# Queries from halves of w_q, and finer key loads at the change of layers, in a two-layer decode kernel

## The chip, the cores and the metric

The kernel runs on one core of one Trainium2 chip. The metric is the device time of one execution in microseconds (us); of the kernel before there are three runs, and their median is taken. All stages below are told in us from the start of the span of one profiled execution.

## The reference

Two equal layers, each an attention block and a feed-forward block, run one decode step for 4 batch entries (B) with model width 512 (D). x is [4, 1, 512] in bf16.

```python
q = layernorm(x) @ wq                       # [4, 512] @ [512, 4096]: 32 query heads of 128
p = softmax(q . k_cache * 128**-0.5)        # 8 key heads, 4 query heads each, 8192 keys
x = x + (p . v_cache) @ wo
h = layernorm(x)
x = x + (silu(h @ w_gate) * (h @ w_up)) @ w_down     # 512 -> 1792 -> 512
# ... and both once more with the same weights and the same caches
```

Nearly all the bytes are the caches: keys and values are 64 MB each, and both layers read them.

## The kernel before, in words

**Tiles.** The work of attention is cut into 16 pairs in each layer; a pair is one batch entry and two key heads. The keys of a pair (here K0 to K15) are 4 MB, 32 KB on each of the 128 partitions, and so are its values (V0 to V15). A tile of this size lies in a slot of the on-chip tensor `kvf`, in 8 blocks of 4 KB a partition. There are four slots (0 to 3), and a fifth one, `QS`, in which w_q lies (4 MB, loaded once as two halves, `wq0` and `wq1`) until layer 1 has made its queries from it; after that QS is a slot as the others. The feed-forward weights are loaded into slot 1 in layer 0 and slot 3 in layer 1.

**One pair.** VectorE (DVE) transposes each block of keys in place (`turn`, L488, 8 instructions). TensorE (PE) makes scores from each block with four matmuls of 512 columns (`scores`, L512). Then DVE takes the maximum (`max_p`, L518), PE turns it (L523), DVE and PE spread it (L526, L549 or L554), ScalarE makes the exponentials (L559), DVE transposes them (L576), and PE multiplies them with the values (`values`, L643).

**Order of the work.** Each engine runs its instructions in the order in which the Python program emits them. Two lists defer work: `blocks` holds score and value blocks until their estimated times exceed a lag, and `line` holds the steps of a softmax. For the second pair of layer 1 the lag is 15 (`AHEAD`), so that all its eight `turn`s stand on DVE ahead of the first pair's `max_p`.

**Order of the loads.** All loads are issued by SyncE (SP), in one fixed list (`cmds`, from L346). `pump` (L405) issues the next command as soon as the program order reaches a point where its blocks are in the set `free`; `freed(s, a, b)` adds blocks a to b of slot s and calls `pump`. Each load waits, on SP, for the readers of the blocks that it writes. A command that isn't ready keeps back all that follow.

**Dependences.** `_Sync` records by name the last writer and the readers of each resource. An instruction waits for the writer of what it reads, and for the writer and the readers of what it writes. The record knows no subset of a name, and no later correction: the writer of `wq0` is whichever instruction last named it in its writes.

**The change of layers.** Layer 0 works through pairs 0 to 15, layer 1 through 15, 14, 13, 12, 0, ... 11. K15 (slot 0, transposed), V15 (slot 3) and V14 (slot 2) stay for layer 1. Blocks 6 and 7 of K13 stay too: `hold` (L444) transposes them into four banks of PSUM in layer 0, and in layer 1 transposes them back into QS (L452), where the rest of K13 is loaded. Because blocks 6 and 7 of QS lie in w_q, the copy back waits for both names `WQ` (L451). In `load`, the first load into QS also takes both of these names as written (L430).

The order at the change is: feed-forward block of layer 0 (`ffn`), `center` (mean and variance), `qproj` (128 small matmuls L839, of which 64 ahead of and 64 behind the variance's matmul L826), then the two copies back, `freed(QS, 0, 6)`, and the pairs. K14 is loaded into slot 1 as the feed-forward weights there are used up, in parts of blocks 0-3 (after w_gate), 3-4 (after w_up) and 4-8 (after w_down). Then come K13 into QS (blocks 0-4 and 4-6), K12 into slot 0 in two halves as the scores of K15 free it, V13 into slot 1 in two halves as the scores of K14 free it, K0 into slot 3 after V15's products, V12 into QS, K1 into slot 2, and so on in a ring of the five slots.

In `qproj`, the matmuls run head by head, with the four parts of D (`kt`) inside; each one reads `wq0` (kt 0, 1) or `wq1` (kt 2, 3).

Of the kernel before, what the change touches and what calls it, by code (L numbers as in the profile page):

```python
# [103 lines left out]
def bass_interleave_layers__gqa_block_cached__swiglu_ffn__decode_kernel(  # L104
# [40 lines left out]
    with ExitStack() as es:  # L145
# [50 lines left out]
        def room(s, a, b):  # L196
            return [f"s{s}.{q}" for q in range(a // BW, (b - 1) // BW + 1)]
# [48 lines left out]
        def bank(k):  # L246
            return ps[:, k * BANKF:(k + 1) * BANKF]
# [87 lines left out]

        ends = lambda it, s: [(it, s, 0, QH), (it, s, QH, NB - 1), (it, s, NB - 1, NB)]
        half = lambda it, s: [(it, s, q, q + NB // 2) for q in range(0, NB, NB // 2)]

        def placed(seq, ring, parts):
            out = []  # L340
            for i, it in enumerate(seq):
                s = ring[i % len(ring)]
                out += parts[i](it, s) if i in parts else [(it, s, 0, NB)]
            return out
# [10 lines left out]

        us = order[1]
        s = W_SLOT[0]
        cmds += [(K(1, us[1]), s, 0, 3), (K(1, us[1]), s, 3, 4), (K(1, us[1]), s, 4, NB)]
        cmds += [(K(1, us[2]), QS, 0, NB // 2), (K(1, us[2]), QS, NB // 2, NB - 2)]
        seq = loads(1, 3)  # L360
        ring = (0, 1, 3, QS, 2)
        cmds += placed(seq, ring, {0: half, 1: half, len(seq) - 1: ends})
        assert W_SLOT[1] == ring[len(seq) % len(ring)]
        cmds += [(("W", 1), W_SLOT[1], 0, NB), (("W+", 1), W_SLOT[1], NB, NB + 1)]

# [58 lines left out]
        def load(it, a, b, sm):  # L424
            kind, L, u = it
            s = slot_of[it]
            gp, bt = pair_gb(u)
            src = (A_k_cache if kind == "K" else A_v_cache)[bt, 2 * gp:2 * gp + 2, :, :].rearrange(
                "h (p t) d -> (h p) (t d)", t=TT)
            over = WQ if s == QS and not q_gone else []  # L430
            q_gone.update(over)
            T.dma("sp", kv[:, s, a * BW:b * BW], src[:, a * BW:b * BW], sm,
                  writes=[f"s{s}.{q}" for q in range(a, b)] + over)
# [398 lines left out]

        def qproj(L, u):
            at, name = place("ln", 0, Hq * B)
            for h in range(Hq):
                if h == Hq // 2:
                    deviation(lsc_sb, "lsc")
                for kt in range(KT):
                    T.op("pe", lambda e: e.matmul(at[:, h * B:(h + 1) * B],  # L839
                                                  lhsT=wq_sb[:, kt, h * Dh:(h + 1) * Dh],  # L840
                                                  rhs=xn[:, kt * B:(kt + 1) * B],
                                                  start=(kt == 0), stop=(kt == KT - 1)),
                         reads=[f"wq{kt // 2}", "xn"], writes=[name], sig=(kt == KT - 1))
            T.op("dve", lambda e: e.tensor_tensor(qT, at.rearrange("p (h b) -> p b h", b=B),
                                                  rstd[:].unsqueeze(2).to_broadcast([P, B, Hq]), ALU.mult),
                 reads=[name, "rstd"], writes=["qT"] + OT)

            pick = ident.rearrange("p (c j e) -> p c j e", c=2, e=2)
            ob, oname = place("q", 0, NQR)
            ob = ob.rearrange("p (c b g r) -> p c b g r", c=4, b=B, g=GP)  # L850
            qv = qT.rearrange("p b (g h r) -> p b g h r", h=2, r=REP)
            for c in range(4):
                for a in range(NA):
                    T.op("pe", lambda e: e.matmul(ob[a * QB:(a + 1) * QB, c],
                                                  lhsT=pick[:, c // 2, :, c % 2],
                                                  rhs=qv[:, :, :, a // 2, :], start=True, stop=True),
                         reads=["qT", "ident"], writes=[oname], sig=(a == NA - 1))
            place_q(L, u, "dve", ob, [oname])
            T.op("dve", lambda e: e.tensor_copy(qr, ob), reads=[oname], writes=["qr", "made"])

        def ffn(L):
            s = W_SLOT[L]
            gb, ub = OBK[0], SBK[0]
            gT = bank(gb)[:, 0:FO * B]
            uT = bank(ub)[:, 0:FO * B]
            fb = lambda ap: ap.rearrange("p (f b) -> p f b", b=B)
            rb = rstd[:].unsqueeze(1).to_broadcast([P, FO, B])
            rooms = {"wg": room(s, 0, O_WU), "wu": room(s, O_WU, O_WD), "wd": room(s, O_WD, O_WD + FO * D)}
            names = {"wg": ["wg"], "wu": ["wu0", "wu1", "wu2"]}
            for at, wname, bk in ((wg_at, "wg", gb), (wu_at, "wu", ub)):  # L870
                for fo in range(FO):
                    if bk == gb and fo == FO // 2:
                        deviation(zero_sb, "zero")
                    f = base(L, fo)
                    for kt in range(KT):
                        T.op("pe", lambda e: e.matmul(bank(bk)[:, fo * B:(fo + 1) * B],  # L876
                                                      lhsT=at(s, kt, *f),
                                                      rhs=xn[:, kt * B:(kt + 1) * B],
                                                      start=(kt == 0), stop=(kt == KT - 1)),
                             reads=rooms[wname] + names[wname] + ["xn"], writes=[f"pb{bk}"],  # L880
                             sig=(fo == FO - 1 and kt == KT - 1))
                freed(s, *((0, 3) if wname == "wg" else (3, 4)))
            T.op("dve", lambda e: e.tensor_tensor(fb(gr), fb(gT), rb, ALU.mult),
                 reads=[f"pb{gb}", "rstd"], writes=["gr", "pb"])
            T.op("act", lambda e: e.activation(eg, gr, ACTF.Exp, scale=-1.0), reads=["gr"], writes=["eg"])
            T.op("dve", lambda e: e.tensor_tensor(fb(gw), fb(gr), rb, ALU.mult), reads=["gr", "rstd"], writes=["gw"])
            T.op("dve", lambda e: e.tensor_scalar(eg, eg, 1.0, None, op0=ALU.add), reads=["eg"], writes=["eg"])
            T.op("dve", lambda e: e.reciprocal(eg, eg), reads=["eg"], writes=["eg"])
            T.op("dve", lambda e: e.tensor_tensor(eg, gw, eg, ALU.mult), reads=["gw", "eg"], writes=["eg"])
            T.op("dve", lambda e: e.tensor_tensor(hT, eg, uT, ALU.mult), reads=[f"pb{ub}", "eg"], writes=["hT"])  # L890
            if L == 1:
                x_rows(1)
                for i, (a, b, _) in enumerate(WDS[1]):
                    for fo in range(a, b):
                        for j in range(NA):
                            o = s * SL + O_WD + fo * D + j * P
                            T.op("pe", lambda e: e.matmul(quarter(j), lhsT=hT[:, fo * B:(fo + 1) * B],
                                                          rhs=kvf[:, o:o + P], start=False, stop=(fo == FO - 1)),
                                 reads=["hT", f"wd{i}"] + rooms["wd"], writes=[f"part{j}"],
                                 sig=(fo == b - 1))  # L900
                freed(s, 4, NB)
                return
            for j, (a, b, _) in enumerate(WDS[0]):
                k = OBK[0] if j else SBK[1]
                for nt in range(KT):
                    for fo in range(a, b):
                        T.op("pe", lambda e: e.matmul(bank(k)[:, nt * B:(nt + 1) * B],
                                                      lhsT=wd_at(s, fo, nt),
                                                      rhs=hT[:, fo * B:(fo + 1) * B],
                                                      start=(j < 2 and nt == 0 and fo == a),  # L910
                                                      stop=(j in (0, NW - 1) and nt == KT - 1 and fo == b - 1)),
                             reads=["hT", f"wd{j}"] + rooms["wd"], writes=[f"pb{k}"], sig=(fo == b - 1))
                if not j:
                    add_to_x(bank(k)[:, 0:XB], f"pb{k}")
            freed(s, 4, NB)
            add_to_x(bank(k)[:, 0:XB], f"pb{k}")


# [10 lines left out]
        for L in range(2):  # L929
# [6 lines left out]
            if L:  # L936
                for q in (NB - 2, NB - 1):
                    hold(q, True)
                freed(QS, 0, NB - 2)
            todo = [("K", 0)]  # L940
            for i in range(1, NP - 1):
                todo += [("K", i), ("V", i - 1)]
# [49 lines left out]
```

## Time and profile before

| | |
|---|---|
| Runs | 648.29, 649.24, 649.81 us, median 649.24 |
| The profiled execution | 648.29 us, of which its span is 646.5 us |
| PE busy | 425.6 us (66%) |
| DVE busy | 430.1 us (67%) |
| ScalarE, GpSimd busy | 41.2 us, 11.1 us |
| Read from memory | 272.90 MB, 422 GB/s over the span |
| Granted TensorE clock, mean | 0.876 |

A busy time is a sum over stages that differ, so it doesn't say by itself which engine sets the end. The page's row of 40 slices shows the share of time in which the 16 DMA engines had packets, and the GB/s that they moved; the chain of waits follows the work that ended last back through whatever released each step. "Landing" is the time from a load's issue on SP until its semaphore is complete. The loads at the change of layers stand like this in the profile, each from SP's own timeline and the landing of that one issue:

| Load | KB | issued at | landed after, us |
|---|---|---|---|
| K14, blocks 0-3 | 1536 | 345.06 | 9.4 |
| K14, 3-4 | 512 | 348.35 | 7.3 |
| K14, 4-8 | 2048 | 351.19 | 9.4 |
| K13, 0-4 and 4-6 | 2048, 1024 | 356.71 and next | 9.0, 11.1 |
| K12, 0-4 | 2048 | 363.87 | 10.6 |
| K12, 4-8 | 2048 | 367.36 | 12.1 |
| V13, 0-4 | 2048 | 372.50 | 11.8 |
| V13, 4-8 | 2048 | 375.98 | 13.2 |
| K0 | 4096 | 378.16 | 20.8 |

### The profile page before, as it was taken

To read this page: it belongs to the slowest core of one execution; us is meant where nothing else is said; L and a number is where in the kernel's file an instruction comes from. 1 tells how busy PE (TensorE), PEld (TensorE's weight loads), DVE (VectorE), ACT (ScalarE), POOL (GpSimd) and SP (SyncE) were. 2 spreads that over 40 slices of the span, in tenths; PEclk is the share of its full clock that TensorE was granted. 3 is DMA by queue.
4 is the path that set the end of the run, shared out by engine and by line. 5 is a ranking of instruction groups with operands and counts; after the bars stand their busy time and mean duration, and the time that the engine had idled before them with its cause. 6 is when DMAs were issued, how large, how long until landed. Compare 5 with 4: busy or idle time off the path is not lost.

```text
span 646.5 us, 7503 instructions
## 1 busy us (share of the span) xinstructions
PE 425.6 (66%) x3128; PEld 173.1 (27%) x3128; DVE 430.1 (67%) x706; ACT 41.2 (6%) x117; POOL 11.1 (2%) x43
## 2 busy tenths in 40 slices
PE   2574466556766755767757987777665576657878
PEld 2221122212322212222226332222222222222225
DVE  1585467566776666777852878888766677766953
ACT  1000000000000000001010010000000000000110
POOL 0000000000000000000000000000000000000000
PEclk9996896789787999878985799999878997789977
DMA  9999999999999999999999999999999999999996
GB/s 363 445 423 416 442 429 430 426 435 433 426 430 435 430 425 436 435 422 436 434 407 409 396 435 434 434 429 423 442 427 426 433 438 424 431 440 423 430 417 268
DMA packets 14129, 273.37 MB, mean 423 GB/s; under 512 B 1416, under 2 KB 1424, under 8 KB 5264
## 3 DMA queue, kind: packets, MB, share of 16 engines
q1 hardware_dynamic: 14096, 272.91, 99.0%
q8 instruction: 24, 0.39, 0.2%
q14 instruction: 9, 0.07, 0.0%
HBM read 272.90 MB, written 0.00 MB: 422 GB/s over the span
## 4 chain that ended last, share of the span: by engine, by line
DMA 61%; DVE 26%; PE 9%; issue 3%; SPq 0%; ACT 0%; DVEq 0%
DMA kvf<-in_A_k_cache_dram 49%; DVE kvf L488 20%; DMA kvf<-in_A_v_cache_dram 10%; PE ps L512 3%; DVE pT L576 3%; PE ps L643 2%; DMA kvf<-in_B_w_down_dram 2%; DVE pb L693 2%; PE ps L839 1%; DVE pb L689 0%; PE ps L876 0%; DVE scr L703 0%; DVE kvf L452 0%; PE ps L759 0%; SPq L93 0%
## 5 line engine op out<-in xcount | busy, mean ns | idle before, releaser
L512 PE MATMUL ps<-kvf,zq 128*128 128x512 bf16 x1024 | 298.0, 426 | 181.1 <-DVE kvf L488 174.3
L488 DVE STREAM_TRANSPOSE kvf<-kvf 128x1024 f32<-128x1024 f32 x246 | 289.8, 1219 | 108.6 <-DMA kvf<-in_A_k_cache_dram 107.7
L512 PEld LDWEIGHTS ps<-kvf,zq 128*128 128x128 bf16 x1024 | 90.6, 105 | 350.9 <-DVE kvf L488 257.8
L643 PE MATMUL ps<-kvf,pT 128*32 128x512 bf16 x960 | 66.7, 400 | 1.4 <-DVE pT L576 0.8
L559 ACT ACTIVATE pb<-ps,tiny 128x512 bf16<-128x512 f32 x32 | 22.0, 688 | 531.8 <-DVE tiny L557 495.2
L576 DVE STREAM_TRANSPOSE pT<-pb 64x512 bf16<-64x512 bf16 x60 | 41.2, 687 | 3.1 <-ACT pb L559 2.0
L518 DVE TENSOR_REDUCE tiny<-ps 128x1 f32<-128x512 f32 x32 | 22.0, 687 | 31.6 <-PE ps L512 31.6
L693 DVE SCALAR_TENSOR_TENSOR pb<-ps,tiny,pb 128x128 f32<-128x128 f32 x104 | 36.5, 351 | 5.1 <-PE ps L643 1.3
L643 PEld LDWEIGHTS ps<-kvf,pT 128*32 128x32 bf16 x960 | 20.8, 98 | 31.9 <-issue 15.7
L698 PEld LDWEIGHTS ps<-sel,pb 128*128 128x128 f32 x64 | 15.4, 258 | 21.3 <-DVE pb L693 14.0
L502 POOL TENSOR_TENSOR zq<-scr,tiny 128x64 bf16<-128x64 bf16 x30 | 9.0, 300 | 564.8 <-PE ps L512 564.8
L526 DVE TENSOR_REDUCE mrm<-ps 1x8 f32<-1x128 f32 x32 | 8.8, 275 | 14.2 <-PE ps L523 14.2
L698 PE MATMUL ps<-sel,pb 128*128 128x8 f32 x64 | 12.7, 272 | 8.1 <-DVE pb L693 8.1
L549 PEld LDWEIGHTS ps<-mrm,tiny 128*128 128x128 f32 x60 | 12.0, 205 | 8.6 <-DVE scr L703 3.2
L759 PE MATMUL ps<-wo_sb,scr 128*4 128x512 bf16 x48 | 11.0, 379 | 1.5 <-DVE scr L728 1.5
L689 DVE TENSOR_SCALAR pb<-ps,tiny 128x128 f32<-128x128 f32 x32 | 10.1, 315 | 2.6 <-PE ps L643 2.6
L549 PE MATMUL ps<-mrm,tiny 128*128 128x16 f32 x60 | 9.3, 231 | 3.1 <-ACT mrm L561 3.1
L839 PE MATMUL ps<-xn,kvf 128*128 128x4 bf16 x256 | 7.6, 166 | 3.8 <-DMA kvf<-in_A_wq_dram 3.0
L561 ACT ACTIVATE mrm<-head,tiny 128x8 f32<-128x8 f32 x32 | 9.6, 301 | 1.0
L523 PE MATMUL ps<-identf,tiny 128*1 128x128 f32 x32 | 8.6, 270 | 0.2 <-DVE tiny L518 0.2
L839 PEld LDWEIGHTS ps<-xn,kvf 128*128 128x128 bf16 x256 | 7.6, 106 | 4.0 <-DMA kvf<-in_A_wq_dram 3.1
L876 PE MATMUL ps<-xn,kvf 128*128 128x4 bf16 x224 | 7.3, 169 | 1.8 <-DMA kvf<-in_B_w_up_dram 1.4
(83 smaller groups left out, 113.9 us busy)
## 6 DMA issues: line engine op xcount, KB each, us to landing
kvf<-in_A_k_cache_dram SPq DMA_DIRECT2D x28, 4096.0 KB, 30.8
kvf<-in_A_v_cache_dram SPq DMA_DIRECT2D x27, 4096.0 KB, 32.9
kvf<-in_A_v_cache_dram SPq DMA_DIRECT2D x4, 2048.0 KB, 20.0
kvf<-in_A_k_cache_dram SPq DMA_DIRECT2D x4, 2048.0 KB, 10.0
kvf<-in_A_wq_dram SPq DMA_DIRECT2D x2, 2048.0 KB, 9.8
wo_sb<-in_A_wo_dram SPq DMA_DIRECT2D x4, 1024.0 KB, 40.6
kvf<-in_B_w_gate_dram SPq DMA_DIRECT2D x2, 1792.0 KB, 24.5
kvf<-in_A_v_cache_dram SPq DMA_DIRECT2D x2, 1536.0 KB, 34.8
```

The costliest lines, as they stand in the source:

```text
L488: T.op("dve", lambda e: e.transpose(w, w), reads=[f"s{s}.{q}"], writes=[f"s{s}.{q}"])
L512: T.op("pe", lambda e: e.matmul(bank(bk)[:, 0:SW], lhsT=zq[:, z0:z0 + P], rhs=w[:, :, c // 2, :, c % 2], start=(q == 0 and c == 0), stop=( ...
L518: T.op("dve", lambda e: e.tensor_reduce(mx[:], bank(bk)[:, 0:SW], AX.X, ALU.max), reads=[f"pb{bk}"], writes=["mx"])
L549: T.op("pe", lambda e: e.matmul(at, lhsT=ones, rhs=mrm[:, i * H2:(i + 2) * H2], start=True, stop=True), reads=[f"m8{i}", "rsm", "onesf"], ...
L559: T.op("act", lambda e: e.activation(pb[:], bank(bk)[:, 0:SW], ACTF.Exp, bias=nm, accum_out=rs), reads=[f"pb{bk}", "nm"], writes=PB + ["rs"])
L576: T.op("dve", lambda e: e.transpose(dst, pb[hp]), reads=["pb", "row"], writes=[name])
L643: T.op("pe", lambda e: e.matmul(bank(k)[j * QB:(j + 1) * QB, q0 * Dh:q1 * Dh], lhsT=p_t[:, t, h, :], rhs=v[:, q0:q1, t, :], start=((last o ...
L689: T.op("dve", lambda e: e.tensor_scalar(into, o, own[:, q:q + 1], None, op0=ALU.mult), reads=[f"pb{k}", "own"], writes=["row"] if last els ...
L693: T.op("dve", lambda e: e.scalar_tensor_tensor(into, o, own[:, q:q + 1], into, op0=ALU.mult, op1=ALU.add), reads=[f"pb{k}", "own", iname], ...
L698: T.op("pe", lambda e: e.matmul(at, lhsT=into, rhs=sel[:], start=True, stop=True), reads=[iname, "sel"], writes=[name])
L759: T.op("pe", lambda e: e.matmul(bank(OUTB)[0:B, 0:D], lhsT=oT[:, h, :], rhs=wo_sb[:, h, :], start=(gp == groups[L][0] and r == 0), stop=(g ...
L839: T.op("pe", lambda e: e.matmul(at[:, h * B:(h + 1) * B], lhsT=wq_sb[:, kt, h * Dh:(h + 1) * Dh], rhs=xn[:, kt * B:(kt + 1) * B], start=(k ...
```

## The change

1. `qproj` runs by halves of w_q: 64 matmuls with kt 0 and 1 over all heads, then the variance, then 64 with kt 2 and 3. One accumulation covers the whole tile: it starts at the first matmul and stops at the last. Between the halves, layer 1 calls `freed(QS, 0, 4)`; after the copies back only blocks 4 to 6 are freed.
2. The first load into each half of QS takes over the name of that half alone.
3. K14 loads as blocks 0-3, 3-4, 4-6, 6-8; w_down's names are kept by part, and blocks 4-6 of slot 1 are freed after the first part of w_down.
4. K12 loads as four parts of two blocks.

```diff
+        twos = lambda it, s: [(it, s, q, q + 2) for q in range(0, NB, 2)]
...
-        cmds += [(K(1, us[1]), s, 0, 3), (K(1, us[1]), s, 3, 4), (K(1, us[1]), s, 4, NB)]
+        cmds += [(K(1, us[1]), s, a, b) for a, b in ((0, 3), (3, 4), (4, 6), (6, NB))]
...
-        cmds += placed(seq, ring, {0: half, 1: half, len(seq) - 1: ends})
+        cmds += placed(seq, ring, {0: twos, 1: half, len(seq) - 1: ends})
...
-            over = WQ if s == QS and not q_gone else []
+            over = [w for i, w in enumerate(WQ) if s == QS and a // (NB // 2) == i and w not in q_gone]
...
-            for h in range(Hq):
-                if h == Hq // 2:
+            for c in range(2):
+                if c:
                     deviation(lsc_sb, "lsc")
-                for kt in range(KT):
...
+                for h in range(Hq):
+                    for kt in (2 * c, 2 * c + 1):
...
+                                                      start=(kt == 0 and h == 0), stop=(kt == KT - 1 and h == Hq - 1)),
+                             reads=[f"wq{c}", "xn"], writes=[name], sig=(kt % 2 == 1 and h == Hq - 1))
+                if L and not c:
+                    freed(QS, 0, NB // 2)
...
-            rooms = {"wg": room(s, 0, O_WU), "wu": room(s, O_WU, O_WD), "wd": room(s, O_WD, O_WD + FO * D)}
+            rooms = {"wg": room(s, 0, O_WU), "wu": room(s, O_WU, O_WD)}
+            for j, (a, b, _) in enumerate(WDS[L]):
+                rooms[f"wd{j}"] = room(s, O_WD + a * D, O_WD + b * D)
...
                 if not j:
+                    freed(s, 4, 6)
                     add_to_x(bank(k)[:, 0:XB], f"pb{k}")
-            freed(s, 4, NB)
+            freed(s, 6, NB)
...
                 for q in (NB - 2, NB - 1):
                     hold(q, True)
-                freed(QS, 0, NB - 2)
+                freed(QS, NB // 2, NB - 2)
```

More of the change, by code (lines that the diff above doesn't have):

```diff
@@ L834, in qproj @@
             at, name = place("ln", 0, Hq * B)
-            for h in range(Hq):
-                if h == Hq // 2:
+            for c in range(2):
+                if c:
                     deviation(lsc_sb, "lsc")
-                for kt in range(KT):
[L839 to L843, printed above, removed]
+                for h in range(Hq):
+                    for kt in (2 * c, 2 * c + 1):
+                        T.op("pe", lambda e: e.matmul(at[:, h * B:(h + 1) * B],
+                                                      lhsT=wq_sb[:, kt, h * Dh:(h + 1) * Dh],
+                                                      rhs=xn[:, kt * B:(kt + 1) * B],
+                                                      start=(kt == 0 and h == 0), stop=(kt == KT - 1 and h == Hq - 1)),
+                             reads=[f"wq{c}", "xn"], writes=[name], sig=(kt % 2 == 1 and h == Hq - 1))
+                if L and not c:
+                    freed(QS, 0, NB // 2)
             T.op("dve", lambda e: e.tensor_tensor(qT, at.rearrange("p (h b) -> p b h", b=B),
@@ L898, in ffn @@
                                                           rhs=kvf[:, o:o + P], start=False, stop=(fo == FO - 1)),
-                                 reads=["hT", f"wd{i}"] + rooms["wd"], writes=[f"part{j}"],
+                                 reads=["hT", f"wd{i}"] + rooms[f"wd{i}"], writes=[f"part{j}"],
                                  sig=(fo == b - 1))
@@ L911, in ffn @@
                                                       stop=(j in (0, NW - 1) and nt == KT - 1 and fo == b - 1)),
-                             reads=["hT", f"wd{j}"] + rooms["wd"], writes=[f"pb{k}"], sig=(fo == b - 1))
+                             reads=["hT", f"wd{j}"] + rooms[f"wd{j}"], writes=[f"pb{k}"], sig=(fo == b - 1))
                 if not j:
+                    freed(s, 4, 6)
                     add_to_x(bank(k)[:, 0:XB], f"pb{k}")
-            freed(s, 4, NB)
+            freed(s, 6, NB)
             add_to_x(bank(k)[:, 0:XB], f"pb{k}")
```

## The prediction

> **What bounds the kernel now.** I read the page's DMA rows first, then the chain, then the change of layers by its chain, SP's issues, DVE's and PE's timelines, and windows.
>
> ```profile
> DMA  9999999999999999999999999999999999999996
> ...
> q1 hardware_dynamic: 14096, 272.91, 99.0%
> ...
> DMA 61%; DVE 26%; PE 9%; issue 3%; SPq 0%; ACT 0%; DVEq 0%
> ```
>
> The loads' packets fill 99.0% of 16 engines' span. Outside the start and the end no slice shows DMA short of work, so the end is when the last bytes are through plus the tail behind them. A delay of any engine costs nothing as long as the DMA queue holds bytes, and everything once it is empty. In layer 1 compute needs less per pair than DMA: after the change of layers it is behind, and from 437.77 it waits for keys again (DVE's timeline, second line below). So I count one thing only: how long the queue stands empty at the change of layers.
>
> The chain there:
>
> ```profile
> 357.64 0.41 DVE scr L859
> 358.06 2.29 DVE kvf L452 x2
> 360.35 9.01 DVE kvf L488 x8
> 369.36 0.59 DVE tiny L518
> 369.99 0.27 PE ps L523
> 370.26 0.87 PE ps L512 x4
> 371.13 0.31 PE ps L554 x2
> 371.44 4.46 PE ps L512 x20
> ```
> ```profile
> 437.77 2.37 DVE L488 STREAM_TRANSPOSE kvf<-kvf 128x1024 f32<-128x1024 f32 x2 [2.38 <-DMA kvf<-in_A_k_cache_dram]
> ```
>
> From 357.98 (DVE's own timeline) DVE copies back K13's blocks 6 and 7 (L452), turns K14's eight blocks (L488), and only then takes K15's maximum (L518). PE has K14's third and fourth block behind the matmul that waits for this maximum (L523). V13's first half is issued when the fourth is scored, at 372.50. So a delay of the copies is a delay of V13's load, one for one.
>
> **The change part by part.**
>
> *Queries by halves.* The same 128 matmuls with 64 ahead of the variance and 64 behind it: nothing in layer 1. In layer 0 the third matmul waits until 13.47 for the second half of w_q; now 64 run in that wait, some 1.8 us of PE. But DVE's first `turn` waits for K0 until 24.25, idle 5.42 us before it: nothing. It would give 1.8 us if keys landed by 17.
>
> *K14's last part cut in two.* Blocks 4-6 can be issued after the first w_down part, at about 349.9 instead of 351.19. The loads in front land until 355.7, so nothing is gained. Three more issues in all, at 0.33 us each on SP, which mostly waits: nothing.
>
> *K13's first half issued between the halves of qproj.* At about 354.5 instead of 356.71. What this can repair is in the windows:
>
> ```profile
> 352.00:356.00 4.00, 3.65 (x114) 3.56 (x114) 0.61 (x4) 0.56 (x2) 0.00 (x0) 0.50 1.04 419
> 356.00:360.00 4.00, 3.27 (x47) 1.62 (x44) 2.79 (x5) 0.00 (x0) 0.00 (x0) 0.50 0.93 336
> ```
>
> The last two columns are DMA's share and GB/s. Share 0.93 over 4 us is 0.3 us lost. By landings, K13's first half came 5.1 us after K14 (360.6 to 365.7), where a full queue takes 4.9 us for 2 MB (379.5 to 384.3 to 389.2). K12's finer parts similarly fill a queue that runs thin around 366. From 360.6 to 379.5 the queue moved 7 MB in 18.9 us; at 4.9 us for 2 MB that is 17.2. So the gain is between 0 and 1.7 us, and without the next step it would be the whole effect of the change.
>
> *The wait that comes with it.* `load` takes over the name `wq0` as its write. Until now this load was issued after the copies back, which wait for both names and so found w_q's own loads, long landed. Now it is issued ahead of them, and the writer of `wq0` is K13's first half. The instruction order of the changed kernel shows it: the first L452 copy on DVE waits for the semaphore of that load, where it waited for w_q's. The copied blocks don't need these bytes; the wait is by name only.
>
> When does it land? K14 lands at 360.6 as before; 2 MB at 4.9 us gives **365.5**. DVE stands still from 357.98 to 365.5: **7.5 us**. Queued behind are the eight turns, K15's maximum, and so PE's third block. PE itself goes on with K15's scores (no need of DVE) until 367.3, so K12's four parts are issued in time, the last at 367.4 as before. They land at 365.5 + 2.5 (K13, 1 MB) + 9.8 (4 MB) = 377.8, or 379.5 if the loss around 370 stays. This is all that the queue holds.
>
> *When V13 comes.* 372.50 + 7.5 = 380.0 if PE runs as fast. But it idles between K14's second block (about 371) and the maximum (369.99 + 7.5 = 377.5), some 6 us. Where that happens now:
>
> ```profile
> 79.35 3.17 PE L512 MATMUL ps<-kvf,zq 128*128 128x512 bf16 x7 [7.63 <-DVE kvf L488]
> ...
> 458.49 3.47 PE L512 MATMUL ps<-kvf,zq 128*128 128x512 bf16 x8 [5.03 <-DVE kvf L488]
> ```
> ```profile
> 76.00:80.00 4.00, 0.65 (x2) 0.28 (x3) 1.95 (x2) 0.00 (x0) 0.00 (x0) 0.50 1.03 442
> ```
>
> After 7.63 us and 5.03 us of idling the granted clock is 0.50 for the first 3.3 us of work (column before DMA's). Four matmuls of a block take 1.03 us at full clock and 1.7 at half (0.43 each in the 358 to 362 stretch). Two blocks: +1.4. V13's first half is issued at **381.4**, between 380.0 and 382.
>
> What it then takes: no row shows a full-size load into an idle queue in mid-run. Bounds: 4.9 us of transfer plus 1.0 from issue to first packet (0.74 to 1.78 in the start's windows) is 5.9; the first half of w_q, issued into the empty queue at the start, landed after 7.8, with DMA slow in its first microseconds (180 and 147 GB/s). I take 7.0, between them. 381.4 + 7.0 = 388.4 against 372.50 + 11.8 = 384.3: **+4.1 us**. The bounds give 380.0 + 5.9 = +1.6 and 382 + 7.8 = +5.5.
>
> *After that.* V13's second half is issued 3.5 to 5 us later, under the first one's transfer. DVE and PE are some 9 us late by then. V12's load goes from 389.06 to 398; K0's, ahead of it, would land at 384.3 + 4.1 + 4.9 + 9.8 = 403.1, so the queue stays filled. Compute's slack of 2.38 us at 437.77 grows by 19.4 (DMA for a pair) less 14.9 (405.46 to 420.15 in the chain) with each pair, so the lag beyond DMA's, 5 us, is gone by 460, and the end moves by DMA's delay alone.
>
> *1 MB loads.* Six are new. K13's 1 MB part, in 8 KB rows, landed 2.5 us after the load in front (365.7 to 368.2), which is the rate of 2 MB parts; I take 0.1 us for all. The Trainium skill's page "DMA: Bandwidth & Descriptors" (section "Measured (HBM→SBUF, 128 partitions, SWDGE, issued from GpSimd)") speaks against the change: a 1 MB transfer takes 6.15 us, 16 MB take 79.0, so it says to batch to 1 MiB and more. By that, six loads would be an estimated 7.3 us dearer than as part of large ones; the row above doesn't bear it out for loads queued behind others.
>
> Sum: stall +4.1, small parts +0.1; the thin places' gain lies ahead of the empty queue and is lost in it. 648.29 + 4.2 = 652.5 for the profiled execution, which was the fastest of the three runs; the median is 0.95 above it. I put the forecast between, **653.0**.
>
> **Rivals.**
> - *The stall is mostly covered* (0.14). If V13 restarts quickly, PE stays at full clock, and the engines whose packets lag (K12's second half was as late as 379.5) have less to lose: +0.8 to +1.6, that is 650 to 651. For: landings there are later than byte counts ask. Against: the queue has nothing behind K12.
> - *Faster* (0.05). One mechanism: the earlier K13 and K12 parts keep the queue full, and the stall ends before the queue does: -1.7, or 647.5. It decides at V13's issue: it must come some 1.5 us before K12's last bytes, by 376, so the stall must stay below 3.5 us, and K13's half land by 361.5. K14, in front of it, lands at 360.6 and 2 MB take 4.9, so this needs the wait not to bind at all.
> - *The queue empties twice* (0.10). If PE stays at half clock for all of K14's last four blocks (16 matmuls, 6.9 us instead of 3.5), V13's second half comes too late as well, and V12's after it: +6 to +9, 654.5 to 658.
> - *Small loads run slow* (0.03). The slowest 2 us with weights in small parts moved 398 GB/s against 430: 6 MB then cost 15.8 us instead of 14.6, +1.2 on top, 654.2. Its rule is the page named above.
> - *The half isn't released early* (0.01): SP would issue K13 as before, without the wait by name: 649.
>
> **How the numbers follow.** The forecast has the rest, 0.67: 651.0 to 654.5 by its bounds. The range takes in the covered stall and part of the double gap: 650.0 to 656.5. About 0.2% (1.3 us) is what a measurement of this kernel can tell from no change. Faster 0.05; within it 0.09 (half of the covered stall, the unreleased half, a little of the forecast's low end); slower 0.86.
>
> **What would show it.** In the changed profile's DVE timeline, an idle time of 7 to 8 us ahead of the first L452, ended by a key load; PE idle some 6 us ahead of L523, and a clock of 0.5 after it; V13's issue at 380 to 382; a window of 2 to 5 us with DMA's share far below 1 between 376 and 384; none of this at 357. Later issues should be 4 to 9 us late, and the keys' wait at 437 should come near 442. I am wrong if the idle time ahead of L452 is missing, or if DMA's share stays near 1 through 376 to 384.

## The result, and the profile after

| | before | after |
|---|---|---|
| Runs, us | 647.47 to 649.81 (5) | 654.68 to 655.70 (5) |
| Median, us | 648.29 | 655.11 |
| The profiled execution (its span) | 648.29 (646.5) | 654.68 (652.9) |
| Ratio after to before | | 1.01, 95% interval 1.0085 to 1.0114 |

The changed kernel is about 1% slower, 6.8 us by the medians. Between the two profiled executions the difference is 6.4 us, in the span as in the whole.

The page of the changed kernel: DMA's busy share in 40 slices, the loads' queue (packets, MB, share of 16 engines' span), and the shares of the chain that ended last.

```profile
DMA  9999999999999999999999959999999999999997
...
q1 hardware_dynamic: 14528, 272.91, 98.1%
...
DMA 62%; DVE 26%; PE 8%; issue 3%; SPq 0%; ACT 0%; ACTq 0%; DVEq 0%
```

The bytes are the same and the share is 98.1% instead of 99.0%. Between the start and the end one digit has changed: slice 24 (375.4 to 391.7 us) fell from 9 to 5. The windows there, with PE, PEld, DVE, ACT and POOL busy, the granted clock, DMA's share and GB/s:

```profile
356.00:360.00 4.00, 3.27 (x49) 1.62 (x47) 0.85 (x3) 0.00 (x0) 0.00 (x0) 0.50 1.03 426
...
372.00:376.00 4.00, 0.00 (x0) 0.00 (x0) 4.00 (x5) 0.00 (x0) 0.00 (x0) 0.91 0.90 371
376.00:380.00 4.00, 2.33 (x7) 0.87 (x7) 1.90 (x3) 0.00 (x0) 0.00 (x0) 0.50 0.11 47
380.00:384.00 4.00, 4.00 (x16) 1.68 (x16) 1.59 (x4) 1.08 (x3) 0.00 (x0) 0.73 0.31 66
384.00:388.00 4.00, 3.81 (x41) 1.30 (x39) 1.79 (x3) 0.00 (x0) 0.30 (x1) 1.00 0.94 401
```

The thin place of before at 356 to 360 (share 0.93) is full, and from 376 to 384 next to nothing is read. What stood in the way is in the chain of the changed kernel (start, us, what):

```profile
354.69 10.94 DMA kvf<-in_A_k_cache_dram
365.63 0.02 issue
365.65 2.38 DVE kvf L453 x2
368.03 9.01 DVE kvf L489 x8
377.04 0.59 DVE tiny L519
377.63 0.04 issue
377.67 0.37 PE ps L524
378.05 1.71 PE ps L513 x4
```

It is the chain of before, moved by 7.6 us, and a load now stands at its head: K13's first half, issued at 354.69 and landed at 365.63. DVE's and PE's own timelines give the idle time ahead of the first copy back and ahead of the matmul that turns K15's maximum (in brackets: idle, and who ended it):

```profile
365.65 2.38 DVE L453 STREAM_TRANSPOSE kvf<-ps 128x1024 f32<-128x1024 f32 x2 [7.49 <-DMA kvf<-in_A_k_cache_dram]
```
```profile
377.67 0.37 PE L524 MATMUL ps<-identf,tiny 128*1 128x128 f32 x1 [6.28 <-DVE tiny L519]
377.84 1.91 PE L513 MATMUL ps<-kvf,zq 128*128 128x512 bf16 x4
```

SP issued V13's first half at 382.17 (372.50 before). It landed 7.3 us later, at 389.4 (384.3 before).

### The profile page after: what moved, and what is told of

The parts are those of the page before. It is cut to its first block, busy times and chain, and to the rows that moved or that the text cites. A ratio compares the mean times of both kernels' runs of the same rounds, so it can differ in the third digit from the quotient of the medians.

```text
span 652.9 us, 7505 instructions
## 1 busy us (share of the span) xinstructions
PE 426.8 (65%) x3126; PEld 174.4 (27%) x3128; DVE 430.2 (66%) x706; ACT 41.2 (6%) x117; POOL 11.2 (2%) x43
## 3 DMA queue, kind: packets, MB, share of 16 engines
q1 hardware_dynamic: 14528, 272.91, 98.1%
## 4 chain that ended last, share of the span: by engine, by line
DMA 62%; DVE 26%; PE 8%; issue 3%; SPq 0%; ACT 0%; ACTq 0%; DVEq 0%
DMA kvf<-in_A_k_cache_dram 49%; DVE kvf L489 19%; DMA kvf<-in_A_v_cache_dram 11%; PE ps L513 3%; DVE pT L577 3%; DVE pb L694 2%; PE ps L644 2%; DMA kvf<-in_B_w_down_dram 2%; DVE pb L690 0%; PE ps L882 0%; DVE kvf L453 0%; DVE ps L456 0%; DVE scr L704 0%; PE ps L524 0%; SPq L93 0%
```

## The experiments

**Theory N**: `hold` waits for the last writer of `wq0`, which is now K13's first half. The copies back stand still for 7.5 us, the turns and K15's maximum behind them are late by as much, V13's load comes when the queue has been empty for some time, and the end moves. **Rival S**: the 1 MB loads are the dear part, or the early load is, by crowding the queue, and the wait is a bystander. All diffs are against the changed kernel; each ratio is against the kernel before, run in the same session (medians 648.62 for e1 to e4, 648.80 for e5 to e7, 648.68 for e8 and e9). The changed kernel's 655.11 is from another session, in which the kernel before had 648.29; a difference taken from 655.11 directly can be off by the 0.3 to 0.5 us between these medians.

### e1: the wait without the name of the first half

```diff
-                 T._wait("dve", T._need((), WQ))
+                 T._wait("dve", T._need((), WQ[1:]))
```

Blocks 6 and 7 lie in the second half of w_q, so the name that is left covers the bytes written.

> The copies back of K13's blocks 6 and 7 wait for the second half of w_q's name alone; all else as in the changed kernel. Theory N (the wait by name is the whole loss): DVE's 7.5 us idle time ahead of the copies is gone, V13's first half is issued at 372 to 373, DMA's share stays at 0.95 or more in every 4 us window from 344 to 392, and the end is 0 to 1.7 us below the kernel before (ratio 0.997 to 1.000). Rival S (the 1 MB loads, or K13's early load itself, cost time): the kernel stays 2 us or more above the kernel before (ratio 1.003 or more) though the idle time is gone.

648.00 us (647.70 to 649.26, 11 runs), ratio 0.999 (0.9981 to 0.9999). DVE's timeline and DMA's windows:

```profile
357.88 2.37 DVE L453 STREAM_TRANSPOSE kvf<-ps 128x1024 f32<-128x1024 f32 x2
360.17 9.09 DVE L489 STREAM_TRANSPOSE kvf<-kvf 128x1024 f32<-128x1024 f32 x8
369.18 0.65 DVE L519 TENSOR_REDUCE tiny<-ps 128x1 f32<-128x512 f32 x1
```
```profile
372.00:376.00 4.00, 4.00 (x26) 1.63 (x28) 1.57 (x3) 0.72 (x3) 0.05 (x1) 1.00 1.03 432
376.00:380.00 4.00, 3.25 (x39) 1.02 (x32) 3.45 (x6) 0.00 (x0) 0.25 (x1) 1.00 1.01 430
```

No bracket, so no idle time; V13 is issued at 372.40, and DMA is full in both windows. Everything else of the change is still in this kernel. The whole loss is therefore tied to one name in one wait, and taken from this kernel it is 655.11 - 648.00 = 7.1 us (7.4 if each is taken against the kernel before of its own session, 6.8 above it and 0.6 below).

### e2: the early load with its wait, coarse parts

```diff
-        cmds += [(K(1, us[1]), s, a, b) for a, b in ((0, 3), (3, 4), (4, 6), (6, NB))]
+        cmds += [(K(1, us[1]), s, a, b) for a, b in ((0, 3), (3, 4), (4, NB))]
...
-        cmds += placed(seq, ring, {0: twos, 1: half, len(seq) - 1: ends})
+        cmds += placed(seq, ring, {0: half, 1: half, len(seq) - 1: ends})
```

> The halves of w_q and K13's early load as changed; K14 and K12 in the coarser parts of before (K14 0-3, 3-4, 4-8; K12 in halves). Theory N: DVE is idle 7.5 us ahead of the copies as in the changed kernel, DMA's share falls to near 0 around 378 to 383, and the end is 5.5 to 7.5 us above the kernel before (ratio 1.0085 to 1.0115). Rival S: with the six 1 MB loads gone a good part of the loss goes too, ratio 1.005 or less.

654.83 us (653.93 to 655.22, 4 runs), ratio 1.0088 (1.0074 to 1.0102): the whole loss, without the finer parts. Its DVE line and its window:

```profile
365.59 2.38 DVE L453 STREAM_TRANSPOSE kvf<-ps 128x1024 f32<-128x1024 f32 x2 [7.42 <-DMA kvf<-in_A_k_cache_dram]
```
```profile
376.00:380.00 4.00, 2.39 (x7) 0.93 (x7) 1.84 (x3) 0.00 (x0) 0.00 (x0) 0.50 0.24 102
```

### e3: the finer parts, without the wait

K13's first half is released after the copies back in the program, as before; the halves of `qproj` and the finer parts stay.

```diff
-                if L and not c:
-                    freed(QS, 0, NB // 2)
...
-                freed(QS, NB // 2, NB - 2)
+                freed(QS, 0, NB - 2)
```

> The finer parts of K14 and K12 and the halves of w_q as changed; K13's first half is released after the copies back, as before. Theory N: no idle time ahead of the copies, V13's first half issued at 372 to 373, the end within 0.2% of the kernel before (ratio 0.998 to 1.001). Rival S: ratio 1.003 or more.

648.00 us (647.70 to 649.32, 11 runs), ratio 0.9991 (0.9982 to 0.9999). But the load itself is not later. SP issues K13's first half at the same time as in the changed kernel (354.69), 2 us ahead of the kernel before (356.71):

```profile
354.65 0.33 SPq L93 DMA_DIRECT2D kvf<-in_A_k_cache_dram  x1
```

The release sets the place of the load in the program, and with it whom the copies find as the writer of `wq0`. When SP issues it is set by the readers it waits for, and these are only the first 64 matmuls of `qproj` (352.70 to 354.57 on PE), since the load takes one half's name. So this kernel has the early load, without the wait. The same two windows as in e1 are full:

```profile
372.00:376.00 4.00, 4.00 (x23) 1.63 (x24) 1.41 (x2) 0.88 (x3) 0.00 (x0) 1.00 1.03 424
376.00:380.00 4.00, 3.24 (x38) 1.03 (x35) 3.48 (x5) 0.00 (x0) 0.30 (x1) 1.00 1.02 434
```

Rival S falls with e1, e2 and e3 together: neither the small loads nor the early load cost anything that can be seen. By each load's first increment in the trace, K12's four 1 MB parts and the part ahead of them came at 365.4, 367.9, 370.4, 372.9 and 375.4 here, 2.5 us apart, half of what 2 MB take. The Trainium skill's page "DMA: Bandwidth & Descriptors" (section "Measured (HBM→SBUF, 128 partitions, SWDGE, issued from GpSimd)") has 6.15 us for a load of 1 MB. The 2.5 us here are another case: SP issued these loads, and they queue behind others.

### e4: PE kept busy in the gap

26 matmuls on w_o, whose result nobody reads, are put ahead of the first `max_t` of layer 1, so that PE does not idle. DVE's wait stays.

```diff
+        late_max = []
...
+            if late_max:
+                late_max.pop()
+                stream(26)
...
+                late_max.append(1)
```

> The changed kernel with 26 matmuls of 512 columns more on PE (on w_o, into a bank that nobody reads) ahead of the one that turns K15's maximum, so that PE works through the time in which it waits for it. Theory N with the clock as a term of its own: the 7.5 us stall stays, the granted clock stays at 1.0 from 377 on, K14's third and fourth blocks take 1.0 us each, V13's first half is issued at 380.4 to 380.9 instead of 382.2, and the end is 1.2 to 1.8 us below the changed kernel's (ratio about 1.008). Rival C: the clock sets nothing that reaches the end: ratio as the changed kernel's, 1.010.

653.36 us (653.20 to 653.60, 4 runs), ratio 1.0067 (1.0052 to 1.0082). PE's timeline:

```profile
377.73 0.27 PE L528 MATMUL ps<-identf,tiny 128*1 128x128 f32 x1 [0.68 <-DVE tiny L520]
377.84 1.03 PE L514 MATMUL ps<-kvf,zq 128*128 128x512 bf16 x4
```

The stall is the same (7.51 us), and the maximum is turned at the same time as in the changed kernel, 377.73 against 377.67. But the four matmuls behind it take 1.03 us instead of 1.91, the granted clock is 1.00 instead of 0.50 in the window 376 to 380, and V13 is issued at 380.24 instead of 382.17. So the clock's share of the loss is 1.9 us at V13's issue, and about as much at the end: 1.75 us by 655.11 - 653.36, and 2.1 by the medians of each session (6.8 against 4.7). The rest stays, as N asks. The Trainium skill's page "TensorE: Matmul & The Clock Gate" (section "Part 1: The HAM clock gate (the "warmup" mystery)") says that the array falls to half clock after an idle window of about 3.4 us; the trace agrees, with 6.28 us of idling and 0.50 after it.

### e5: a smaller dose of the same wait

K13's first half comes as two loads of 1 MB, and the first of them takes over the name `wq0`, so that the copies wait for 1 MB instead of 2.

```diff
-        cmds += [(K(1, us[2]), QS, 0, NB // 2), (K(1, us[2]), QS, NB // 2, NB - 2)]
+        cmds += [(K(1, us[2]), QS, 0, 2), (K(1, us[2]), QS, 2, 4), (K(1, us[2]), QS, NB // 2, NB - 2)]
```

> K13's first half is loaded as two loads of 1 MB, so that the name wq0 is written by the first of them and the copies back wait for half as many bytes; all else as changed. Theory N with the empty queue as its price: the first MB lands at about 363.2, 2.4 us earlier than the half (365.6); DVE's idle time falls from 7.5 to 5.1 us, V13's first half is issued at about 379.8 instead of 382.2 and lands at about 387.1, and the end is 2.4 us below the changed kernel's (ratio about 1.0063): one for one, since the queue is empty from 378 on in both. Rival P (the price is a fixed one of a broken order, not a length): the end stays within 1 us of the changed kernel's, ratio 1.0085 or more.

653.12 us (652.05 to 653.47, 4 runs), ratio 1.0062 (1.0049 to 1.0075). Its DVE line:

```profile
363.28 2.38 DVE L453 STREAM_TRANSPOSE kvf<-ps 128x1024 f32<-128x1024 f32 x2 [5.11 <-DMA kvf<-in_A_k_cache_dram]
```

The stall is 2.38 us shorter, V13's issue (379.79) 2.38 us earlier, the end 2.0 us earlier (2.5 by the medians of each session, 6.8 against 4.3): dose and effect nearly one for one.

### e9: a dose smaller again

The first part is one block of 512 KB.

```diff
-        cmds += [(K(1, us[2]), QS, 0, NB // 2), (K(1, us[2]), QS, NB // 2, NB - 2)]
+        cmds += [(K(1, us[2]), QS, 0, 1), (K(1, us[2]), QS, 1, NB // 2), (K(1, us[2]), QS, NB // 2, NB - 2)]
```

> The first part of K13, which takes over the name of the first half of w_q, is one block of 512 KB instead of four. Theory N by one for one: 512 KB land 1.3 us after K14, near 361.9, so DVE stands still for about 3.8 us, PE idles 5 us and is still at half clock after it, V13 is issued near 378.4, and the end is at 651.5 to 652.0 us. If the bytes that are queued cover a stall of this length, V13's landing is less than 1.5 us later than in the kernel before, and the end is at 648.5 to 650 us.

651.57 us (650.79 to 652.92, 6 runs), ratio 1.0046 (1.0033 to 1.0060). The line:

```profile
362.01 2.38 DVE L453 STREAM_TRANSPOSE kvf<-ps 128x1024 f32<-128x1024 f32 x2 [3.91 <-DMA kvf<-in_A_k_cache_dram]
```

V13 is issued at 378.53. Stalls of 7.5, 5.1 and 3.9 us cost 6.8, 4.3 and 2.9 us by the medians (655.11 - 648.29, 653.12 - 648.80, 651.57 - 648.68). A stall of 3.9 us is still not covered by the bytes that are queued. Smaller ones were not tried.

### e6: the same wait, with nothing late behind it

The wait is left as the changed kernel has it. The copies back, and the release of blocks 4 to 6, are moved behind K14's eight turns.

```diff
+            if L and u == order[1][1]:
+                for q in (NB - 2, NB - 1):
+                    hold(q, True)
+                freed(QS, NB // 2, NB - 2)
...
-            if L:
-                for q in (NB - 2, NB - 1):
-                    hold(q, True)
-                freed(QS, NB // 2, NB - 2)
```

> The changed kernel with its wait by name left as it is, but the two copies back stand on DVE behind K14's eight transposes instead of ahead of them. Theory N (a wait costs only what is queued behind it): K14's transposes run from 358 to 367.1, K13's half has landed at 365.6 by then, so DVE doesn't idle at all ahead of the copies; K15's maximum comes at 369.4, V13's first half at 372 to 373, and the end is that of the kernel whose copies wait for the second half's name alone (648.0, ratio 0.998 to 1.000). Rival W (the wait or the early load itself is the loss, wherever it stands): ratio 1.005 or more.

648.01 us (647.74 to 649.22, 12 runs), ratio 0.999 (0.9982 to 0.9999). DVE's timeline:

```profile
358.10 9.12 DVE L489 STREAM_TRANSPOSE kvf<-kvf 128x1024 f32<-128x1024 f32 x8
367.14 2.34 DVE L453 STREAM_TRANSPOSE kvf<-ps 128x1024 f32<-128x1024 f32 x2
369.40 0.65 DVE L519 TENSOR_REDUCE tiny<-ps 128x1 f32<-128x512 f32 x1
```

The copies still need K13's load by name, but they come at 367.14, when it has landed. What cost time was the wait at the head of an engine that runs in order, ahead of work that did not need it.

### e7: the early load, coarse parts, without the wait

e2 with e1's line: coarse parts, K13's first half early, copies that wait for the second half's name only.

> The halves of w_q and K13's early load, K14 and K12 in the coarser parts of before, and the copies back wait for the second half's name alone. It is what the early load is worth by itself. If it fills the thin place at 357 to 359 and this reaches the end: 0.3 to 0.6 us below the kernel before, ratio 0.999 or less. If the finer parts alone give what the two together gave (both 648.0): within 0.05% of the kernel before, ratio 0.9995 to 1.0005.

647.93 us (647.48 to 649.33, 12 runs), ratio 0.9989 (0.9981 to 0.9998), no idle time ahead of the copies. Against e2, the wait by name costs 654.83 - 647.93 = 6.9 us here, as the 7.1 us above.

### e8: the release after the copies, coarse parts

e2's and e3's edits together: K13's first half released after the copies back in the program, coarse parts.

> Queries by halves, but neither the early load of K13 nor the finer parts. If the two load edits brought the 0.6 to 0.9 us by which e1, e3, e6 and e7 beat the kernel before, this one equals the kernel before: 648.5 to 649.0 us, ratio within 0.0005 of 1, and DMA's share between 356 and 360 us falls below 0.95 again, as in the kernel before. If the halves of the queries brought it, it comes out at 648.0 us, ratio 0.999, with that window full.

648.22 us (647.25 to 649.52, 11 runs), ratio 0.9996 (0.9987 to 1.0006). This doesn't decide what it was made for: its interval holds both the kernel before and the 648.0 of the others. Its edit doesn't leave out the early load, either. As in e3, SP issues K13's first half early, and the window behind it is full:

```profile
354.81 0.33 SPq L93 DMA_DIRECT2D kvf<-in_A_k_cache_dram  x1
```
```profile
356.00:360.00 4.00, 3.27 (x54) 1.76 (x52) 2.56 (x5) 0.00 (x0) 0.00 (x0) 0.50 1.00 414
```

So e8 is in effect e7 again: the same loads at nearly the same times, without the wait. Its expectation, that the window falls below 0.95 again, took the program's order for the time of issue. In all ten kernels that have the halves of `qproj`, K13's first half is issued at 354.5 to 354.8 and this window has a share of 1.00 or more; the kernel before, with 356.71 and 0.93, is the only one without. This agrees with the thin place being filled by the earlier load, though only one profile, that of the kernel before, shows it unfilled.

**Where the gain of the edits went.** e1, e3, e6 and e7 beat both kernels, by 0.6 to 0.9 us against before; the intervals of their ratios end at 0.9998 or 0.9999. They cannot be told from each other, and hardly from e8, so it stays open how much of it each edit brings. All five have the early load and no wait that costs; they differ in K14's and K12's parts. By the table below, V13's first bytes are complete at 381.3 in the kernel before, at 380.9 and 381.6 with the coarse parts (e7, e8), and at 379.9 to 380.3 with the fine ones (e1, e3, e6). So at the change of layers the fine parts stand at least 0.6 us ahead, while the early load by itself shows no gain beyond the 0.7 us by which e7 and e8 differ. At the end the fine parts' lead is not seen: 648.00, 648.00 and 648.01 with them, 647.93 and 648.22 without.

**Where the loss reaches the end.** The trace has 16 increments of the semaphore for each of these loads, as many as there are DMA engines. It doesn't name the engine; I read them as one for each. The table gives the landing of V13's first half, and of the first part of layer 1's last values, by the first and by the last of the 16 increments, with the span of the same execution, in us:

| Kernel | V13, first | spread to last | last V, first | spread to last | span |
|---|---|---|---|---|---|
| before | 381.3 | 3.0 | 624.2 | 4.5 | 646.5 |
| after | 388.9 | 0.5 | 631.8 | 3.1 | 652.9 |
| e1 | 379.9 | 2.8 | 622.8 | 5.5 | 646.0 |
| e2 | 389.0 | 0.4 | 631.9 | 3.1 | 653.2 |
| e3 | 380.3 | 2.6 | 623.2 | 4.7 | 645.9 |
| e4 | 387.1 | 0.4 | 629.9 | 3.4 | 651.6 |
| e5 | 386.5 | 0.5 | 629.4 | 3.4 | 651.0 |
| e6 | 380.2 | 2.8 | 623.1 | 5.2 | 646.4 |
| e7 | 380.9 | 2.6 | 623.8 | 4.3 | 646.0 |
| e8 | 381.6 | 2.3 | 624.7 | 3.6 | 646.2 |
| e9 | 385.4 | 0.3 | 628.6 | 3.1 | 651.1 |

Between the two loads the first engine takes 242.9 to 243.2 us in all eleven: the steady stretch gives nothing back and adds almost nothing. The end follows the last engine: from its landing to the end of the span it is 17.8 to 18.4 us in ten of the kernels (19.4 in e9, whose profiled execution was the slowest of its six), where from the first engine's it is 21.1 to 23.3. So the loss is 388.9 - 381.3 = 7.6 us of standing still, less 1.5 because the slowest engine trails by 3.06 instead of 4.53, plus 0.3 behind that load: 6.4 us.

## Why the prediction was right, and where its sizes were off

The mechanism came as described, and the total was too small: +3.8 us was forecast (from 649.24, the median of the runs known then, to 653.0), and the medians measured later are 6.8 apart. 655.11 us lies above the 651.0 to 654.5 that the forecast's own bounds gave. It is inside the wider range only because that range took in part of a rival, the queue that empties twice, which did not happen; that the range held is luck to this extent.

- **What bounds the kernel**: right. DMA's empty time at the change of layers is the loss, and the table's 242.9 us in both kernels show that nothing behind it gave time back or took more, apart from the engines' spread.
- **The wait by name**: right in place, cause and size. Forecast landing 365.5, measured 365.63; forecast stall 7.5, measured 7.49. e1 and e6 show that it is this wait and what is queued behind it.
- **V13's issue**: 381.4 forecast, 382.17 measured. The maximum was turned 7.68 us late (369.99 to 377.67), 0.2 more than the stall. The **clock term** was the one under-sized: 1.4 forecast, from two blocks at half clock; measured 1.9 by e4. Four matmuls took 1.91 us, not the 1.7 reckoned, and the small ones between the blocks were slow too.
- **A 2 MB load into an empty queue**: 7.0 forecast, chosen between two far bounds; 7.3 measured, and 7.2 in e2, e4 and e5.
- Together these make V13's landing +5.1 where the prediction had **+4.1** (0.8 from the issue, 0.3 from the load, rounded). That lies inside its bounds of +1.6 to +5.5, close to the upper one.
- **"The end moves by DMA's delay alone"**: right, but the delay was read from the last engine's landing. In the old kernel that landing came 3.0 us behind the first engine's, and in the new one 0.5, and it is 0.3 to 0.5 in all five kernels in which the queue ran empty. Then the spread grows by 2.5 us to layer 1's last values, against 1.5 in the old kernel. So 1.0 us of the loss does not show at V13 and comes back later. This is the step that fell short: the term "+4.1" had one landing stand for 16 engines. With 0.3 behind it, the sum is 6.4 (5.1 + 1.0 + 0.3) instead of 4.2.
- **What costs nothing**: right for the halves of `qproj` and K14's parts, by e1 and e3, which hold both and lose nothing, and e8. The 0.1 us for small loads was not seen. The thin places' gain is lost in the empty queue as said; without the wait it is at most 0.6 to 0.9 us at the end, inside the 0 to 1.7 given.
- **What brings K13's load forward**: issue forecast at 354.5, measured 354.69, but the prediction put it down to the release between the halves. e3 (354.65) and e8 (354.81) have it without that release: the halves of `qproj`, with one name per half, are enough. The release moved forward brought only the wait.
- **The rivals**: the covered stall would have left PE at full clock; e4 shows that even then 4.7 us remain (653.36 - 648.62). The faster kernel needed a stall below 3.5 us, in effect no wait; e9's 3.9 us still cost 2.9, and e1 without the wait came out at 648.0, not at 647.5. The second gap did not come: V13's second half was issued 3.57 us behind the first (382.17, 385.74), and the share is 0.94 from 384. Small loads that run slow are excluded by e1 and e3.
- **What would show it**: the idle times, the clock and the windows came as listed. V13's issue, at 382.17, lies just behind the 380 to 382, and V12's, 9.7 us late (389.06 to 398.80), just above the 4 to 9. One sign was wrong. The keys' wait of 437 was to come near 442, but no wait is there; compute was still behind, and DVE's first wait for keys after the change of layers is this one:

```profile
463.75 2.37 DVE L489 STREAM_TRANSPOSE kvf<-kvf 128x1024 f32<-128x1024 f32 x2 [3.67 <-DMA kvf<-in_A_k_cache_dram]
```

The idle time begins at 460.1. It fits the prediction's own estimate that the lag is gone by 460, which the 442 contradicted.

## What to carry to other kernels

When an issue is moved ahead of an instruction in the program, look up who that instruction now waits for: a tracker that knows resources by name takes the new writer, also where the bytes are others, and on an engine that runs in order all that is queued behind pays. Look up as well what the load itself waits for: here the move did not make it any earlier (354.69 with it, 354.65 and 354.81 without), so it could have been left out. Price such a stall at the next load that it delays, against the time when what is queued runs out: here 7.5 us of waiting cost 6.4, of which the restarted PE at half clock made about 1.8, and moving the two copies behind the work that did not need the load (e6) made the same wait free. Measure a DMA delay at the first of its engines as well as at the last, since here the levelled engines hid 1.0 us of the delay.

## What the runs showed of the hardware that was not expected

**The 16 DMA engines drift apart, and an empty queue levels them.** This rests on reading the 16 increments as the 16 engines. In the old kernel the last engine was 1.6 us behind the first at 366.6, 3.0 at 371.5, 3.9 at 599.9 and 4.5 at 619.3. The growth comes in steps of 0.5 to 1.4 us, while the first engine keeps 9.7 us for each 4 MB load. The steps fall near the loads of instructions, which have a queue of their own in the page of the changed kernel:

```profile
q8 instruction: 24, 0.39, 0.2%
```

These are 24 packets of 16 KB; each took 0.9 to 1.1 us in the trace. In the old kernel one stands at 372.0: in the load that was under way then, 15 engines end within 1.6 us and the sixteenth 1.4 us after them. The next steps, at 599.9 and 619.3, have packets at 588.1 and 620.5 near them. Against it, the load that was under way at 588.1 still landed with a spread of 2.99, and the six packets between 394.4 and 553.3 left the spread at 3.0. The trace does not name a packet's engine, and no experiment moved these loads, so the cause is only suggested. Whatever it is, it can swallow a small gain: at the last values e1's first engine was 1.4 us earlier than in the old kernel, its last one 0.4 us.
